# A fused gated recurrence and maxout layer: w_out fetched in two halves, and block 0's second layer split by unit halves around its first layer

## The chip, the cores and the metric

The kernel runs on one core of a Trainium2 chip. The metric is the device time of one launch in microseconds (us), as the median of repeated executions of the same program. Beside it there is one profiled execution with a trace of every instruction of the five engines: TensorE (PE, matrix products; PEld is its weight load), VectorE (DVE), ScalarE (ACT), GpSimd (POOL, here almost only an issuer of DMAs) and SyncE (SP, an issuer of DMAs).

## The reference

What is computed is a recurrence over time for each of four sequences of 6144 tokens and 256 channels, followed by a two-branch maxout layer on every token:

```python
sig = 1 / (1 + exp(-f_logit))
f = lower_bound + (1 - lower_bound) * sig
i = 1 - f
for t in range(S):                       # S = 6144, batch 4, 256 channels
    h = f[:, t] * h + i[:, t] * x[:, t]
    y[:, t] = h
h1 = y @ w1                              # 256 -> 1024
h2 = y @ w2
out = maximum(h1, h2) @ w_out            # 1024 -> 256
```

The kernel uses max(h1, h2) = h1 + relu(h2 - h1). So the first layer multiplies by wd, made of w2 - w1; the second layer multiplies the relu's result by w_out, and adds y times w13, the product of w1 and w_out, which is made once on the chip.

## The kernel before

Time is cut into blocks of 512 tokens. The 24576 tokens make 48 blocks; the first sequence begins with four blocks that are fetched singly (block 0 even in two halves by SP, lines 113 to 123), the rest in chunks of 1024 that go through a scratch buffer and are transposed by the DMA (`cross`, line 143). For each block:

- the gate: ACT takes the sigmoid of the turned logits (`gate`, L201; for block 0 inside `first_recurrence`, L252);
- the recurrence: DVE makes the decay (L207), the drive (L217) and scans them (L224; block 0 L258), which gives y with channels on the partitions;
- the first layer (`first_layer`, L434): 1024 units as eight groups `fc` of 128, two matmuls of 512 tokens each. Two groups share a PSUM tile `dT`, of which there are two in turn, and ACT's relu (L442) empties a tile into `rts`, half precision;
- the second layer (`second_layer`, L480): for each of four groups of 128 tokens, ten matmuls of 256 columns into one PSUM tile: two of y with `w13`, eight of the relu's groups with `wob` (w_out in half precision). When two token groups are done, ACT or DVE copies them to `osb` and SP stores the block (`store`, L453).

From block 4 on, pairs of blocks use seven products in place of eight for the second layer (`sevenths`, L643); that part isn't touched. Its parts t1 to t4 are made of `wob` and `w13` by `make_sevens` (L413).

The order of instructions on each engine is the order of the calls in the program, written out by hand; there is no scheduler. An engine runs its instructions in that order, and waits where an operand or a buffer isn't ready. PSUM has the two `dT` tiles (pool `ps_d`) and four `ps` tiles (pool `ps_o`).

The opening, lines 657 to 750, is where the change lies. In order:

- SP issues the loads of block 0 in two halves, then of w1 and w2, each in two halves `g` of 512 units (`fetch_w`): w1 half 0, w2 half 0, w1 half 1, w2 half 1.
- POOL waits for the first half of w1 (`pool_waits`, L341), then issues the load of w_out in one DMA (L666, it converts to half precision), the loads of blocks 1 to 3 (L105) and of the first scratch chunk (L100).
- PE keeps busy with transposes of a constant (`warm_up`, L678) between the turns of block 0's halves (L136).
- w1's half g is scaled (`scale_w1`, L345, ACT) and cast (`half_w1`, L349: half 0 on ACT, half 1 on DVE); PE turns it (`turn_w1`, L376), and DVE keeps the turned copy as `w1T` (`keep_w1T`, L382). `make_wd` (L358, DVE) makes the first-layer weights from w2 and the scaled w1, in pairs of unit groups.
- Block 0's first layer for units 0 to 3 needs half 0 alone, for units 4 to 7 half 1.
- `make_w13` (L390) is two products of eight matmuls, one for each 128 channels; ACT copies each to `w13` (L397).
- Block 1's logits and x are turned by PE (`turn`, L174), 8 transposes each; block 1's recurrence follows on ACT and DVE.
- Block 0's second layer runs as eight slots of five matmuls, between which stand block 2's turns and the first matmuls of block 1's first layer.

From block 2 on, PE alternates two matmuls of a block's first layer with five of the second layer of the block before.

Of the kernel before, what the change touches and what calls it, by code (L numbers as in the profile page):

```python
# [9 lines left out]
FP32 = mybir.dt.float32  # L10
# [8 lines left out]
def kernel(  # L19
# [76 lines left out]
    def fetch(c, s):  # L96
        b, t0, nt, _ = chunks[c]
        src = srcs[s][b, t0 : t0 + nt, :]
        if by_xbar(c, s):
            nc.gpsimd.dma_start(  # L100
                out=pieces(scratch[s][c % NSCR][:]), in_=pieces(src)
            )
        else:
            nat = inpool.tile([P, TB // P, D], HALF, name=("fT", "xT")[s])
            nc.gpsimd.dma_start(  # L105
                out=nat[:].rearrange("p i d -> p (i d)"),
                in_=src.rearrange("(p i) d -> p (i d)", p=P),
            )
            held[c, s] = nat
# [87 lines left out]
    def gate(j):  # L197
        new_mid(j, ("u",))
        u = mids[j, "u"]
        fT = turned[j, 0]  # L200
        nc.scalar.activation(  # L201
            out=like(u[:, :, 0:TB], fT), in_=fT, func=AF.Sigmoid, scale=-1.0
        )
# [40 lines left out]
    def first_recurrence(k):  # L244
        nt = TB // 2
        cols = slice(k * nt, (k + 1) * nt)
        if k == 0:
            new_mid(0, ("u", "ff", "v"))
            new_block(0)
        u, ff, v = (mids[0, t] for t in ("u", "ff", "v"))  # L250
        fT, xT = raws[k, 0], raws[k, 1]
        nc.scalar.activation(  # L252
            out=like(u[:, :, cols], fT), in_=fT, func=AF.Sigmoid, scale=-1.0
        )
        decay(ff, u, cols)
        drive(v, u, xT, cols)
        for h in range(KC):
            nc.vector.tensor_tensor_scan(  # L258
                out=y_of(0, h)[:, cols],
                data0=ff[:, h, cols],  # L260
                data1=v[:, h, cols],
                initial=y_of(0, h)[:, nt - 1 : nt] if k else 0.0,
                op0=ALU.mult,
                op1=ALU.add,
            )
# [49 lines left out]
    lbr = const.tile([KC, P], FP32)  # L315
    waited = const.tile([P, 1], FP32)
    warm = const.tile([P, 1], FP32)
    wob = wpool.tile([P, FC, D], HALF)
    wd = wpool.tile([P, KC, DFF], HALF)
    w1T = wpool.tile([P, FC, D], HALF)  # L320
    w13 = wpool.tile([P, KC, D], HALF)
# [18 lines left out]
    def pool_waits(t):  # L340
        nc.gpsimd.tensor_copy(out=waited[:], in_=t)  # L341

    def scale_w1(g):
        for kc in range(KC):
            nc.scalar.mul(w1s[g][:, kc, :], w1n[g][:, kc, :], om[:, kc : kc + 1])  # L345

    def half_w1(g, copy):
        for kc in range(KC):
            copy(out=w1h[g][:, kc, :], in_=w1s[g][:, kc, :])  # L349
# [19 lines left out]
        g, q = divmod(fc, NQ)  # L369
        return slice(g * NQ * P + q, (g + 1) * NQ * P, NQ)  # L370

    def turn_w1(g):
        pt = ps_o.tile([P, NQ, KC, P], HALF, name="ps")
        for q in range(NQ):
            for kc in range(KC):
                nc.tensor.transpose(  # L376
                    pt[:, q, kc, :], w1h[g][:, kc, q : NQ * P : NQ], ident[:]
                )
        return pt

    def keep_w1T(g, pt):
        nc.vector.tensor_copy(  # L382
            out=w1T[:, g * NQ : (g + 1) * NQ, :],
            in_=pt[:].rearrange("p q k d -> p q (k d)"),
        )

    def make_w13(kc):
        psw = ps_o.tile([P, 2, D], FP32, name="ps")
        for fc in range(FC):
            nc.tensor.matmul(  # L390
                psw[:, 0, :],
                lhsT=w1T[:, fc, kc * P : (kc + 1) * P],
                rhs=wob[:, fc, :],
                start=(fc == 0),
                stop=(fc == FC - 1),
            )
        nc.scalar.copy(out=w13[:, kc, :], in_=psw[:, 0, :])  # L397

# [1 line left out]

    def right(k, cols):

        return wob[:, k * KH : (k + 1) * KH, cols], w13[:, k, cols]

    def make_sevens():
        b11, b12, b21, b22 = (right(k, c) for k in range(2) for c in (lo, hi))
# [19 lines left out]
    def first_layer(j, fc):  # L428
        k, g = divmod(fc, KH)
        if fc % 2 == 0:  # L430
            dts["d"] = ps_d.tile([P, 2, TB], FP32, name="dT")
        dT = dts["d"]
        for kc in range(KC):
            nc.tensor.matmul(  # L434
                dT[:, fc % 2, :],
                lhsT=wd[:, kc, unit_cols(fc)],
                rhs=y_of(j, kc),
                start=(kc == 0),
                stop=(kc == KC - 1),
            )  # L440
        if fc % 2:
            nc.scalar.activation(  # L442
                out=rts[j, k][:, g - 1 : g + 1, :].rearrange(
                    "p q (i m) -> p q i m", m=P
                ),
                in_=dT[:].rearrange("p q (m i) -> p q i m", m=P),
                func=AF.Relu,
            )

    def store(j, osb, groups=slice(0, TB // P), cols=slice(0, D), queue=None):  # L450
        b, t0, nb, c, o = blocks[j]
        r0 = b * S + t0
        (queue or nc.sync).dma_start(  # L453
            out=out[r0 : r0 + nb, :].rearrange("(p n) d -> p n d", p=P)[
                :, groups, cols
            ],
            in_=osb[:, groups, cols],
        )
# [3 lines left out]
    def second_layer(j, slot):  # L462
        ns = TB // P
        n = KC + FC
        total = ns * n
        for k in range(slot * total // FC, (slot + 1) * total // FC):
            i, s = divmod(k, n)
            g, r = divmod(i, 2)
            if s == 0 and r == 0:
                acc["ps"] = ps_o.tile([P, 2, D], FP32, name="ps")  # L470
                if i == 0:
                    acc["osb"] = opool.tile([P, TB // P, D], FP32, name="osb")
            ps, osb = acc["ps"], acc["osb"]
            toks = slice(i * P, (i + 1) * P)
            if s < KC:
                left, right = y_of(j, s)[:, i:TB:ns], w13[:, s, :]
            else:
                fc = s - KC
                left, right = rts[j, fc // KH][:, fc % KH, toks], wob[:, fc, :]
            nc.tensor.matmul(  # L480
                ps[:, r, :],
                lhsT=left,
                rhs=right,
                start=(s == 0 and r == 0),
                stop=(s == n - 1 and r == 1),
                skip_group_check=True,
            )
            if r == 1 and s == n - 1:
                (nc.scalar.copy if j in (0, 3) else nc.vector.tensor_copy)(
                    out=osb[:, 2 * g : 2 * g + 2, :], in_=ps[:]  # L490
                )
                if i == ns - 1:
                    store(j, osb)

    sums = {}

# [160 lines left out]
    with tc.manual_schedule():  # L657
# [4 lines left out]
        fetch_first(1)  # L662
        for g in range(NG):
            fetch_w(g)
        pool_waits(w1n[0][:, 0, 0:1])
        nc.gpsimd.dma_start(  # L666
            out=wob[:].rearrange("p (g q) c -> p g (q c)", g=NG),
            in_=moe_w_out.rearrange("(g p q) c -> p g (q c)", g=NG, q=NQ),
        )
        for c in range(1, 5):  # L670
            for s in range(2):
                fetch(c, s)
        wt = ps_d.tile([P, 2, 2 * TB], HALF, name="dT")
        lbc = ps_d.tile([P, TB], FP32, name="dT")

        def warm_up(n):
            for q in range(n):
                nc.tensor.transpose(wt[:, 0, 0:P], ident[:], ident[:])  # L678
# [18 lines left out]
        first_turn(1, 0)  # L697
        first_turn(1, 1)
        first_recurrence(1)
        warm_up(24)  # L700
        scale_w1(0)
        half_w1(0, nc.scalar.copy)
        scale_w1(1)
        pt0 = turn_w1(0)
        for pair in range(2):
            make_wd(0, pair)
            for fc in range(2 * pair, 2 * pair + 2):
                first_layer(0, fc)
        half_w1(1, nc.vector.tensor_copy)
        pt1 = turn_w1(1)  # L710
        for pair in range(2):
            make_wd(1, pair)
            for fc in range(4 + 2 * pair, 6 + 2 * pair):
                first_layer(0, fc)
        keep_w1T(0, pt0)
        keep_w1T(1, pt1)
        steps = turn_steps(1)
        make_w13(0)
        turn(steps[:8])
        gate(1)  # L720
        make_w13(1)
        turn(steps[8:])
        for step in scan_steps(1):
            step()
        cross(4)
        for fc in range(FC):
            if fc == 4:
                turn(turn_steps(2))
                gate(2)
            if fc == 6:  # L730
                first_layer(1, 0)
                first_layer(1, 1)
            if fc < 7:
                second_layer(0, fc)
        for step in scan_steps(2):
            step()
        for step in make_sevens():
            step()
        for fc in range(2, FC):
            first_layer(1, fc)  # L740
            if fc == 3:
                second_layer(0, 7)
        turn(turn_steps(3))
        gate(3)
        early = scan_steps(3)
# [106 lines left out]
```

## Time and profile before

| | |
|---|---|
| median of 5 executions | 379.16 us |
| lowest to highest | 378.44 to 380.36 us |
| the profiled execution, its own time | 378.44 us |
| its span, first to last instruction | 376.7 us |
| time around the span | 1.7 us |
| mean granted clock of TensorE | 0.999 |
| DVE, ACT, POOL busy | 90%, 80%, 12% of the span |
| first matmul of block 0's first layer | 11.11 us |
| first matmul of block 2's first layer | 27.49 us |
| w_out, issue to landing | 6.2 us |

The profiled execution is the lowest of the five. Lines of the trace are read as: start, length, engine, source line, operation, what is written from what is read (buffer numbers left out), shapes, how many in a row; in brackets, how long the engine had been idle before and what ended that. A matmul's length covers its latency, and the next one starts before it ends, so the pace of PE is read from one start to the next.

### The profile page before, as it was taken

What the parts mean: (1) busy time and instruction counts of PE and PEld (TensorE: products, weight loads), DVE (VectorE), ACT (ScalarE), POOL (GpSimd) and SP (SyncE); (2) the same over time, 40 slices, a digit from 0 to 9 for tenths busy, and PEclk for the clock granted to TensorE, in tenths of its full rate; (3) what the DMA queues carried; (4) which work ended last, traced back from release to release, by engine and by line L of the source; (5) the groups of instructions that cost most, each with busy time, mean ns of one, the idle gap of its engine ahead of it and who ended that gap; (6) DMA issues with size and microseconds to landing.
All of it is one profiled execution on the core that took longest, in us unless ns stands there. A gap on an engine that the chain in (4) does not pass through costs nothing.

```text
span 376.7 us, 9634 instructions
## 1 busy us (share of the span) xinstructions
PE 369.4 (98%) x4156; PEld 281.9 (75%) x4156; DVE 338.1 (90%) x408; ACT 303.2 (80%) x412; POOL 43.6 (12%) x80
## 2 busy tenths in 40 slices
PE   7999999999999999999999999999999999999995
PEld 6777767777777777777777777777777777777784
DVE  5796889999999999999999999999999999999762
ACT  5866798888888798798888888887988888888752
POOL 1402101201102012011022021010110220110000
PEclk9999999999999999999999999999999999999999
DMA  8999979999999799799999998999997999992223
GB/s 267 241 209 233 271 131 221 220 178 269 211 140 260 126 273 240 158 279 198 195 238 211 197 292 140 218 276 140 258 274 143 250 219 180 232 183 86 114 111 114
DMA packets 104543, 77.17 MB, mean 205 GB/s; under 512 B 93298, under 2 KB 95348, under 8 KB 103796
## 3 DMA queue, kind: packets, MB, share of 16 engines
q1 hardware_dynamic: 101536, 51.19, 61.8%
q0 software_dynamic: 2544, 25.17, 35.4%
q8 instruction: 32, 0.52, 0.6%
q10 hardware_dynamic: 420, 0.20, 0.2%
q14 instruction: 11, 0.09, 0.1%
HBM read 53.48 MB, written 48.23 MB: 270 GB/s over the span
## 4 chain that ended last, share of the span: by engine, by line
PE 96%; DMA 1%; SPq 0%; DVE 0%; ACT 0%; issue 0%; DVEq 0%
PE ps L643 45%; PE dT L434 44%; PE ps L480 5%; DMA osb<-in_x_dram 1%; PE ps L174 1%; PE dT L678 1%; PE ps L390 0%; SPq L117 0%; PE ps L376 0%; DVE osb L561 0%; ACT nat L128 0%; PE ps L136 0%; DVE osb L582 0%; ACT sn L574 0%; PE dT L643 0%
## 5 line engine op out<-in xcount | busy, mean ns | idle before, releaser
L442 ACT ACTIVATE r<-dT 128x1024 f16<-128x1024 f32 x192 | 196.1, 1023 | 52.3 <-PE dT L434 52.1
L434 PE MATMUL dT<-r,wd 128*128 128x512 f16 x768 | 225.1, 379 | 0.0
L643 PEld LDWEIGHTS <-S 128*128 128x128 f16 x1760 | 115.5, 101 | 37.2 <-DVE S L499 0.2
L643 PEld LDWEIGHTS <-r 128*128 128x128 f16 x1320 | 90.9, 101 | 36.9 <-issue 0.2
L224 DVE TENSOR_TENSOR_SCAN r<-ff,r,v 128x512 f16<-128x512 f16 x88 | 108.2, 1269 | 0.8
L643 PE MATMUL ps<-t,S 128*128 128x128 f16 x1320 | 101.6, 219 | 0.0
L499 DVE TENSOR_TENSOR S<-r 128x2560 f16<-128x2560 f16 x44 | 65.4, 1487 | 14.3 <-ACT r L442 14.1
L434 PEld LDWEIGHTS <-wd 128*128 128x128 f16 x768 | 67.7, 113 | 4.8 <-DVE wd L358 0.6
L643 PE MATMUL ps<-wob,r 128*128 128x128 f16 x704 | 69.9, 219 | 0.0
L499 DVE TENSOR_TENSOR S<-r,S 128x2560 f16<-128x2560 f16 x44 | 64.9, 1475 | 0.0
L279 ACT ACTIVATE u<-fT 128x512 f16<-128x512 f16 x88 | 56.1, 637 | 1.3 <-DMA fT<-scr 1.3
L341 POOL CAST waited<-fT 128x1 f32<-128x1 f16 x22 | 17.8, 809 | 284.4 <-DMA fT<-scr 284.4
L207 DVE TENSOR_SCALAR ff<-u,nom 128x512 f16<-128x512 f16 (+1 forms) x98 | 31.8, 345 | 9.8 <-ACT u L279 3.9
L643 PE MATMUL ps<-w,r 128*128 128x128 f16 x176 | 38.5, 219 | 0.0
L643 PE MATMUL ps<-t,r 128*128 128x128 f16 x430 | 34.1, 219 | 0.1
L561 DVE TENSOR_TENSOR osb<-ps,sn 128x512 f32<-128x512 f32 x44 | 30.1, 684 | 3.2 <-PE ps L643 3.2
L643 PE MATMUL ps<-wob,S 128*128 128x128 f16 x352 | 32.6, 219 | 0.0
L217 DVE TENSOR_TENSOR v<-u,xT 128x1024 f16<-128x1024 f16 x44 | 30.1, 684 | 0.0
L549 ACT COPY sn<-ps 128x512 f32<-128x512 f32 x44 | 25.8, 586 | 2.0 <-PE ps L643 2.0
L559 ACT COPY osb<-ps 128x512 f32<-128x512 f32 x43 | 25.1, 583 | 0.8 <-PE ps L643 0.8
L480 PEld LDWEIGHTS <-r 128*128 128x128 f16 x160 | 16.0, 101 | 6.6
L643 PE MATMUL ps<-w,S 128*128 128x128 f16 x88 | 19.3, 219 | 0.0
(58 smaller groups left out, 136.2 us busy)
## 6 DMA issues: line engine op xcount, KB each, us to landing
out_dram<-osb SPq DMA_DIRECT2D x46, 512.0 KB, 4.3
scr<-in_f_logit_dram POOLq DMA_DIRECT2D x22, 512.0 KB, 7.5
scr<-in_x_dram POOLq DMA_DIRECT2D x22, 512.0 KB, 10.3
r<-in_moe_w_dram SPq DMA_DIRECT2D x4, 512.0 KB, 6.4
fT<-in_f_logit_dram POOLq DMA_DIRECT2D x3, 256.0 KB, 8.3
xT<-in_x_dram POOLq DMA_DIRECT2D x3, 256.0 KB, 8.9
out_dram<-osb SPq DMA_DIRECT2D x3, 256.0 KB, 2.5
osb<-in_f_logit_dram SPq DMA_DIRECT2D x2, 256.0 KB, 3.0
```

What stands on the lines that cost most here:

```text
L207: nc.vector.tensor_scalar(out=ff[:, h, cols], in0=u[:, h, cols], scalar1=nom[:, h : h + 1], scalar2=1.0, op0=ALU.mult, op1=ALU.add,)
L217: nc.vector.tensor_tensor(out=like(v[:, :, cols], xT), in0=like(u[:, :, cols], xT), in1=xT, op=ALU.mult,)
L224: nc.vector.tensor_tensor_scan(out=y_of(j, h), data0=ff[:, h, o : o + TB], data1=v[:, h, o : o + TB], initial=0.0 if t0 == 0 else y_of(j - ...
L279: nc.scalar.activation(out=mids[p + NBLK, "u"][:, h, cols], in_=held[c, 0][:, h, cols], func=AF.Sigmoid, scale=-1.0,)
L434: nc.tensor.matmul(dT[:, fc % 2, :], lhsT=wd[:, kc, unit_cols(fc)], rhs=y_of(j, kc), start=(kc == 0), stop=(kc == KC - 1),)
L442: nc.scalar.activation(out=rts[j, k][:, g - 1 : g + 1, :].rearrange("p q (i m) -> p q i m", m=P), in_=dT[:].rearrange("p q (m i) -> p q i ...
L480: nc.tensor.matmul(ps[:, r, :], lhsT=left, rhs=right, start=(s == 0 and r == 0), stop=(s == n - 1 and r == 1), skip_group_check=True,)
L499: nc.vector.tensor_tensor(out=t[:], in0=a, in1=b, op=op)
L549: nc.scalar.copy(out=t[:], in_=bank[b][:])
L559: nc.scalar.copy(out=dst, in_=bank[b][:])
L561: nc.vector.tensor_tensor(out=dst, in0=bank[b][:], in1=snap[name][:], op=ALU.add)
L643: nc.tensor.matmul(bank[b][:, i, :], lhsT=a[:, k, cols], rhs=w, start=fresh, stop=after is not None, skip_group_check=True,)
```

## The change

Four things change, all in the opening.

1. `wob` becomes two tiles, one for each half of the units, each loaded by a DMA of its own. POOL waits for block 0's second gate (the last column of the first half of `mids[0, "u"]`) in place of the first half of w1, and the loads that POOL issues come after that point.
2. The scaling of w1's half 1 moves from ACT, where it stood ahead of block 0's relus, to DVE, after the turned half 0 has been kept. `keep_w1T` of each half moves ahead.
3. Block 0's second layer runs in a new function, `second_first`: after the first layer's units 0 to 3 it multiplies their relu with the first half of w_out for all four token groups, into two PSUM tiles that stay open; only then is half 1 of w1 turned and are units 4 to 7 computed. The y part and units 4 to 7 follow after `make_w13`, for three token groups in a row and a fourth after block 2's logits have been turned. Both copies to `osb` are ACT's. The relu of units 6 and 7 of block 0 moves to DVE.
4. `make_w13` writes both its products into one `dT` tile in place of two `ps` tiles; the order of it, of block 1's turns and of block 2's turns changes as shown. Block 1's first layer runs its units 2 to 7 without second-layer matmuls between.

```diff
-    wob = wpool.tile([P, FC, D], HALF)
+    wob = [wpool.tile([P, KH, D], HALF, name=f"wob{g}") for g in range(2)]
...
-    def scale_w1(g):
+    def scale_w1(g, mul):
         for kc in range(KC):
-            nc.scalar.mul(w1s[g][:, kc, :], w1n[g][:, kc, :], om[:, kc : kc + 1])
+            mul(w1s[g][:, kc, :], w1n[g][:, kc, :], om[:, kc : kc + 1])
...
     def make_w13(kc):
-        psw = ps_o.tile([P, 2, D], FP32, name="ps")
+        if kc == 0:
+            dts["w"] = ps_d.tile([P, 2, TB], FP32, name="dT")
+        psw = dts["w"][:, kc, :]
         for fc in range(FC):
             nc.tensor.matmul(
-                psw[:, 0, :],
+                psw[:, 0:D],
                 lhsT=w1T[:, fc, kc * P : (kc + 1) * P],
-                rhs=wob[:, fc, :],
+                rhs=wob[fc // KH][:, fc % KH, :],
                 start=(fc == 0),
                 stop=(fc == FC - 1),
             )
-        nc.scalar.copy(out=w13[:, kc, :], in_=psw[:, 0, :])
+        nc.scalar.copy(out=w13[:, kc, :], in_=psw[:, 0:D])
...
         if fc % 2:
-            nc.scalar.activation(
...
-                func=AF.Relu,
-            )
+            dst = rts[j, k][:, g - 1 : g + 1, :].rearrange("p q (i m) -> p q i m", m=P)
+            src = dT[:].rearrange("p q (m i) -> p q i m", m=P)
+            if j == 0 and fc == FC - 1:
+                nc.vector.tensor_scalar_max(out=dst, in0=src, scalar1=0.0)
+            else:
+                nc.scalar.activation(out=dst, in_=src, func=AF.Relu)
...
+    def open_first():
+        acc["first"] = [ps_o.tile([P, 2, D], FP32, name="ps") for g in range(2)]
+        acc["osb0"] = opool.tile([P, TB // P, D], FP32, name="osb")
+
+    def second_first(i, fcs, y=False):
+        ns = TB // P
+        g, r = divmod(i, 2)
+        ps, osb = acc["first"][g], acc["osb0"]
+        toks = slice(i * P, (i + 1) * P)
+        terms = [(y_of(0, s)[:, i:TB:ns], w13[:, s, :]) for s in range(KC) if y]
+        terms += [
+            (rts[0, fc // KH][:, fc % KH, toks], wob[fc // KH][:, fc % KH, :])
+            for fc in fcs
+        ]
+        for n, (left, right) in enumerate(terms):
+            nc.tensor.matmul(
+                ps[:, r, :],
+                lhsT=left,
+                rhs=right,
+                start=(fcs[0] == 0 and r == 0 and n == 0),
+                stop=(fcs[-1] == FC - 1 and n == len(terms) - 1),
+                skip_group_check=True,
+            )
+        if fcs[-1] == FC - 1 and r == 1:
+            nc.scalar.copy(out=osb[:, 2 * g : 2 * g + 2, :], in_=ps[:])
+            if i == ns - 1:
+                store(0, osb)
...
-        pool_waits(w1n[0][:, 0, 0:1])
-        nc.gpsimd.dma_start(
-            out=wob[:].rearrange("p (g q) c -> p g (q c)", g=NG),
-            in_=moe_w_out.rearrange("(g p q) c -> p g (q c)", g=NG, q=NQ),
-        )
-        for c in range(1, 5):
-            for s in range(2):
-                fetch(c, s)
...
         first_recurrence(1)
+        pool_waits(mids[0, "u"][:, 0, TB - 1 : TB])
+        for g in range(NG):
+            nc.gpsimd.dma_start(
+                out=wob[g][:].rearrange("p q c -> p (q c)"),
+                in_=moe_w_out[g * NQ * P : (g + 1) * NQ * P, :].rearrange(
+                    "(p q) c -> p (q c)", q=NQ
+                ),
+            )
+        for c in range(1, 5):
+            for s in range(2):
+                fetch(c, s)
         warm_up(24)
-        scale_w1(0)
+        scale_w1(0, nc.scalar.mul)
         half_w1(0, nc.scalar.copy)
-        scale_w1(1)
         pt0 = turn_w1(0)
         for pair in range(2):
             make_wd(0, pair)
             for fc in range(2 * pair, 2 * pair + 2):
                 first_layer(0, fc)
+        keep_w1T(0, pt0)
+        scale_w1(1, nc.vector.tensor_scalar_mul)
         half_w1(1, nc.vector.tensor_copy)
-        pt1 = turn_w1(1)
+        pt1 = new_pt()
+        open_first()
+        for fcs in ((0, 1), (2, 3)):
+            for i in range(TB // P):
+                second_first(i, fcs)
+        turn_w1(1, pt1)
         for pair in range(2):
             make_wd(1, pair)
+            if pair:
+                keep_w1T(1, pt1)
             for fc in range(4 + 2 * pair, 6 + 2 * pair):
                 first_layer(0, fc)
-        keep_w1T(0, pt0)
-        keep_w1T(1, pt1)
         steps = turn_steps(1)
-        make_w13(0)
         turn(steps[:8])
         gate(1)
+        make_w13(0)
+        turn(steps[8:])
         make_w13(1)
-        turn(steps[8:])
         for step in scan_steps(1):
             step()
         cross(4)
-        for fc in range(FC):
-            if fc == 4:
-                turn(turn_steps(2))
-                gate(2)
-            if fc == 6:
-                first_layer(1, 0)
-                first_layer(1, 1)
-            if fc < 7:
-                second_layer(0, fc)
+        last = tuple(range(KH, FC))
+        for i in range(3):
+            second_first(i, last, True)
+        steps = turn_steps(2)
+        turn(steps[:8])
+        gate(2)
+        second_first(3, last, True)
+        first_layer(1, 0)
+        first_layer(1, 1)
+        turn(steps[8:])
         for step in scan_steps(2):
             step()
         for step in make_sevens():
             step()
         for fc in range(2, FC):
             first_layer(1, fc)
-            if fc == 3:
-                second_layer(0, 7)
```

More of the change, by code (lines that the diff above doesn't have):

```diff
@@ L370, in unit_cols, with new_pt, turn_w1 @@
         return slice(g * NQ * P + q, (g + 1) * NQ * P, NQ)
-    def turn_w1(g):
-        pt = ps_o.tile([P, NQ, KC, P], HALF, name="ps")
+    def new_pt():
+        return ps_o.tile([P, NQ, KC, P], HALF, name="ps")
+    def turn_w1(g, pt=None):
+        pt = pt or new_pt()
         for q in range(NQ):
@@ L396, in make_w13 @@
             )
-        nc.scalar.copy(out=w13[:, kc, :], in_=psw[:, 0, :])
+        nc.scalar.copy(out=w13[:, kc, :], in_=psw[:, 0:D])
     lo, hi = slice(0, P), slice(P, 2 * P)
     def right(k, cols):
-        return wob[:, k * KH : (k + 1) * KH, cols], w13[:, k, cols]
+        return wob[k][:, :, cols], w13[:, k, cols]
     def make_sevens():
@@ L441, in first_layer @@
         if fc % 2:
[L442 to L446, printed above, removed]
-                func=AF.Relu,
-            )
+            dst = rts[j, k][:, g - 1 : g + 1, :].rearrange("p q (i m) -> p q i m", m=P)
[4 more added lines that the diff above has]
+                nc.scalar.activation(out=dst, in_=src, func=AF.Relu)
     def store(j, osb, groups=slice(0, TB // P), cols=slice(0, D), queue=None):
@@ L478, in second_layer @@
                 fc = s - KC
-                left, right = rts[j, fc // KH][:, fc % KH, toks], wob[:, fc, :]
+                left, right = rts[j, fc // KH][:, fc % KH, toks], wob[fc // KH][:, fc % KH, :]
             nc.tensor.matmul(
@@ L488, in second_layer @@
             if r == 1 and s == n - 1:
-                (nc.scalar.copy if j in (0, 3) else nc.vector.tensor_copy)(
+                (nc.scalar.copy if j == 3 else nc.vector.tensor_copy)(
                     out=osb[:, 2 * g : 2 * g + 2, :], in_=ps[:]
```

## The prediction

> **What bounds the kernel now.** I read the page first: its busy shares, then the chain that ended last.
>
> ```profile
> PE 369.4 (98%) x4156; PEld 281.9 (75%) x4156; DVE 338.1 (90%) x408; ACT 303.2 (80%) x412; POOL 43.6 (12%) x80
> ...
> PE 96%; DMA 1%; SPq 0%; DVE 0%; ACT 0%; issue 0%; DVEq 0%
> ```
>
> PE is 98% busy, and 96% of the chain is PE work. A busy PE need not be PE at its peak, so I next read PE's order of time over the opening, where the change sits (start us, length, instruction, count; starts minus starts give the pace).
>
> ```profile
> 10.46 0.81 PE L376 MATMUL ps<-ident,S 128*128 128x128 f16 x8
> 11.11 1.91 PE L434 MATMUL dT<-r,wd 128*128 128x512 f16 x8
> 12.85 0.61 PE L376 MATMUL ps<-ident,S 128*128 128x128 f16 x8
> 13.30 1.98 PE L434 MATMUL dT<-r,wd 128*128 128x512 f16 x8
> 15.12 1.06 PE L390 MATMUL ps<-wob,w1T 128*128 128x256 f16 x8
> 16.02 0.61 PE L174 MATMUL ps<-ident,fT 128*128 128x128 f16 x8
> 16.46 1.04 PE L390 MATMUL ps<-wob,w1T 128*128 128x256 f16 x8
> 17.34 0.61 PE L174 MATMUL ps<-ident,xT 128*128 128x128 f16 x8
> 17.78 0.49 PE L480 MATMUL ps<-w,r 128*128 128x256 f16 x2
> ...
> 27.49 0.59 PE L434 MATMUL dT<-r,wd 128*128 128x512 f16 x2
> ```
>
> Eight L434 take 12.85 - 11.11 = 1.74, 0.217 each; eight L390 0.87, 0.109 each; eight transposes 0.44. From 12.85 to 27.49 (block 2's first matmul) work stands back to back. I count only some 0.25 us lost: 0.09 in the second L434 group, 0.03 after each L390 group, 0.11 at 17.78, where the second matmul waits for w13. So reordering can recover at most 0.25 there and 0.16 at 10.46 (the transposes wait for ACT's S): 0.4 us, 0.1% of the run.
>
> ACT and DVE beside it, then POOL:
>
> ```profile
> 10.84 1.34 ACT L345 ACTIVATE r<-r,om 128x512 f32<-128x512 f32 x2 [0.20 <-DMA r<-in_moe_w_dram]
> 12.19 1.94 ACT L442 ACTIVATE r<-dT 128x1024 f16<-128x1024 f32 x2
> ...
> 17.58 0.37 ACT L397 CAST w<-ps 128x256 f16<-128x256 f32 x1
> ```
>
> ```profile
> 10.40 1.65 DVE L358 SCALAR_TENSOR_TENSOR wd<-r,om 128x256 f16<-128x256 f32 x4
> 11.98 0.74 DVE L349 CAST S<-r 128x512 f16<-128x512 f32 x2
> 12.65 1.66 DVE L358 SCALAR_TENSOR_TENSOR wd<-r,om 128x256 f16<-128x256 f32 x4
> 14.24 1.27 DVE L382 COPY w1T<-ps 128x1024 f16<-128x1024 f16 x2
> ```
>
> ```profile
> 8.44 0.87 POOL L666 DMA_DIRECT2D wob<-in_moe_w_out_dram  x1
> ...
> 14.94 0.50 POOL L100 DMA_DIRECT2D scr<-in_x_dram  x1 [1.57 <-DMA wob<-in_moe_w_out_dram]
> ```
>
> The reader should see: the first relu starts at 12.19 and a relu takes 1.02 (pitch 0.92); w1's second half has just landed at 10.84; w_out, issued at 8.44, lands 6.2 later (14.64), first needed at 15.12.
>
> **What the Trainium skill says.** "TensorE: Matmul & The Clock Gate", Back-to-back issue gap: N/2.4 + 2.5 ns when warm, 216 ns for 512 columns and 109 for 256; the trace agrees (217, 109). So moving matmuls changes no price. "VectorE: DVE Perf Modes", The perf-mode tier table: tensor_scalar on fp32 in SBUF runs at twice the base rate, with an fp32 PSUM operand at the base rate; the errata table above it gives 120 + FD cycles at 0.96 GHz from PSUM. The trace agrees for the like of both: DVE's fp32 cast of 512 (L349) takes 0.41, and L217 reading 1,024 from PSUM 1.22. "DMA: Bandwidth & Descriptors", Issuing engines are not separate DMA queues: all DMAs share 16 engines and interleave. The trace shows the sharing, though little interleaving at first: between 8 and 10 us the SP queue alone fills 105% of them, and POOL's w_out packets first appear after 10.25.
>
> **The change, part by part.** PE's matmuls are the same: block 0's second layer was 40 of L480, and is 16 + 24. So the sum is of waits added and removed, on the clock of the profiled execution. Until 12.85 nothing differs: warm_up(24), the turn of w1's first half and units 0-3 keep their places, and relu 0-1 waits for its matmuls (4 issued by 11.76, the last ending 0.38 later, 12.14), so taking L345 off ACT gains it 0.05 at most.
>
> 1. First half amid the first layer. At 12.85 PE turned w1's second half; now it wants relu 0-1: 12.18 + 1.02 = 13.20, issue 13.25. Wait 0.40. Eight matmuls to 14.12; relu 2-3 ends 13.10 + 1.02 = 14.12: wait 0.05. Eight more to 15.04.
>
> 2. w_out. POOL now waits for block 0's second gate (ACT 7.35, 0.59 long: 7.94) instead of w1 (8.30), so the issue starts at about 8.15, and each half takes about the 0.55 of an fT issue. Queued behind it on POOL: the six fT/xT fetches, shifted under 0.3, and block 1's fT is needed at 17.23 instead of 16.02. Half 0's landing is not in the trace. Upper bound: whole w_out's landing, 14.64, less the second half's 0.26 MB at the 0.43 MB per 2 us that POOL's queue moves from 12 to 14 us (1.2): 13.45. Lower: less also the 0.6 by which its issue ends earlier (8.70 for 9.31), if the engines take it up at once: 12.85. Needed 13.25. I take a wait of 0.1 beyond step 1 (0 to 0.25).
>
> 3. w1's second half on DVE. After wd (11.98): keep_w1T 0.60 (half of 1.27 less overlap), scale two at pitch 0.34 as L349, or 0.6 if at base rate, cast 0.67: S ready at 14.0 to 14.5; PE turns it at 15.04. No wait. wd pair 0 by 14.8 to 15.3, first layer needs it at 15.48; pair 1 by 15.6 to 16.1, needed 16.35. Free, by up to 0.2. keep_w1T of half 1 ends about 16.4, before 17.67. Units 4-7: 15.48 to 17.23.
>
> 4. Relu 6-7 on DVE: matmuls end at 17.39, (120 + 1,024)/0.96 = 1.19 by the skill's table (L217 1.22), done 18.65. Next there is block 1's decay, which waits for gate(1) until 18.9. Hidden; if it grew by over 0.25 it would push block 1's scans, which end at 23.2 against a need at 23.64.
>
> 5. w13. Turn f 17.23-17.67; make_w13(0) 17.67-18.54; turn x to 18.98. Both products now use one dT tile, and in the changed program's instruction list the second product's first matmul waits for ACT's copy of the first. ACT: gate(1) from 17.87, pitch 0.92, copy 18.79-19.16. PE resumes 19.21: wait 0.23. make_w13(1) then issues to 20.08, ends 20.24; copy 20.28-20.65. In the kernel before, eight transposes covered this copy (17.34-17.78, and still 0.11 waited). Now second_first follows directly; only one y matmul (w13's first half) can go ahead, so the second issues at 20.70: wait 0.51. Seventeen more matmuls to 22.55.
>
> 6. Turn f(2) to 22.99, second_first(3) to 23.64, block 1 units 0-1 to 24.51, turn x(2) to 24.95. gate(2) follows the first osb copy, 23.2; second osb copy 24.12; relu 0-1 24.67; units 2-3 issue to 25.82, relu 2-3 26.02-27.04. Units 4-5 go to 26.69; units 6-7 need the dT buffer that relu 2-3 frees: 27.08, wait 0.39. Before, L480 work between the pairs (23.14, 24.33) hid this. Then to 27.95, turn(3) to 28.84, block 2 starts.
>
> Stores: block 0's leaves from the same place in SP's queue; cross(4)'s transposes still wait for the same two scr loads. DVE afterwards: scans of block 2 end 28.9, the sevens (1.95) 30.85, block 3's scans about 35.7, needed at 36.64. Late, not on the path.
>
> Sum: added 0.40 + 0.05 + 0.10 + 0.23 + 0.51 + 0.39 = 1.68; removed 0.25. Net +1.4 (28.84 - 27.49 = 1.35 without the w_out term). PE is full from there to the end, so nothing recovers it. The profiled execution took 378.44, 376.7 of it span; it becomes 379.9. It is the lowest of five, 0.72 under their median of 379.16; against the median the same 1.4 gives 380.6.
>
> **Rivals.**
> - Not slower: the executions that the profile doesn't show. Before, w1's second half was awaited by ACT at 10.84, and S was done 0.13 before PE wanted it (12.72 to 12.85): a landing over about 0.13 later stalls PE. After, S has 0.5 to 1 to spare. If that is what makes the median 0.72 longer than the profiled run, the change returns it: 380.6 - 0.7 = 379.9, no measurable change; at the highest run's 1.92, 378.7, faster. For it: the spread of the runs, and both cover margins. Against: w_out's half 0 is equally tight after, at 13.25, and w_out itself had only 0.5 before.
> - Half 0 of w_out is late: it shares engines with w1 and w2, and if it lands only with the whole at 14.64, PE waits 1.4 at 13.25 instead of 0.05 to 0.4; +1.1 more, 381.7. For: the SP queue is served until about 12. Against: half the bytes come first.
> - The waits don't carry: PE later proves paced by DVE (90% busy) or by buffers, and absorbs the shift: 379.2. For: DVE above 95% in the 200-300 us stage. Against: PE's busy equals the span in every stage from 13 to 300 us. I put unknown effects of either sign here too.
>
> **How the numbers follow.** Main case 0.50: 380.6, own range 380.0 to 381.2. Not slower by better cover 0.22, late half 0.15, no carry or unknown 0.13. A measurement tells about 0.3%, 1.14 us, from no change: slower means above 380.30. Main case: 0.36 slower, 0.14 within. Cover: 0.17 within, 0.05 faster. Late half: 0.15 slower. Last: 0.07 within, 0.06 faster. Together faster 0.11, same 0.38, slower 0.51. The range 379.2 to 381.7 holds all of the main case, most of the cover case and the smaller late halves, 0.8 in all.
>
> **What would show it.** In the changed profile: PE waits on ACT's relu before the first second-layer matmul (0.4), on a w13 copy between the two products (0.2) and after the second (0.5), and on relu 2-3 before block 1's units 6-7 (0.4); block 2's first matmul at 28.8 to 29.0 instead of 27.49; S on DVE before 14.6. A wait named w_out above 0.3 is the late half. If block 2 starts within 0.3 of 27.49, or if the end is not shifted as block 2's start is, my sum is wrong.

## The result, and the profile after

The changed kernel takes 380.24 us (median of 43 executions, 379.25 to 383.76), the kernel before 379.28 us in the comparison (80 executions, 377.9 to 382.71). The ratio is 1.0025, with a 95% interval of 1.0013 to 1.0038: slower, by 0.96 us, where 1.4 was forecast. The interval is 0.5 to 1.44 us, so it just holds the forecast as well.

The profiled execution of the changed kernel took 382.14 us and is one of its longest. Its span is 380.3. Its page, with busy time and the chain that ended last:

```profile
PE 368.3 (97%) x4156; PEld 280.5 (74%) x4156; DVE 340.3 (89%) x411; ACT 301.2 (79%) x409; POOL 42.9 (11%) x81
...
DMA 57%; PE 34%; issue 3%; POOL 2%; DVE 1%; ACT 1%; SPq 0%; POOLq 0%; DVEq 0%
```

The chain has turned from 96% PE to 57% DMA, and that misleads. Followed back from the end it reaches one place near 292 us where PE waited for a DVE copy that was late behind a chunk's x (the first line below is PE's waits after 45 us, the second DVE's order of time):

```profile
PE ps L677 <- DVE osb L595: 1.1, 1, 1.1
```

```profile
287.44 0.69 DVE L217 TENSOR_TENSOR v<-u,xT 128x1024 f16<-128x1024 f16 x1 [2.50 <-DMA xT<-scr]
```

From there the chain follows scratch transfers back to the start, although PE waited for none of the others. It is one late transpose (8.97 us from its issue, where the median of all 22 is 5.2), and hardly a trait of the changed kernel: a variant of the kernel before, with another input for block 1, had such a wait too, of 1.5 us. So the profile of the changed kernel was taken once more among the experiments, and that one is read here. It took 379.99 us, its span is 378.2. PE's order of time over the opening:

```profile
11.19 1.89 PE L439 MATMUL dT<-r,wd 128*128 128x512 f16 x8
13.46 1.91 PE L516 MATMUL ps<-wob,r 128*128 128x256 f16 x16 [0.39 <-DMA wob<-in_moe_w_out_dram]
15.21 0.61 PE L379 MATMUL ps<-ident,S 128*128 128x128 f16 x8
15.65 1.89 PE L439 MATMUL dT<-r,wd 128*128 128x512 f16 x8
17.38 0.61 PE L174 MATMUL ps<-ident,fT 128*128 128x128 f16 x8
17.83 1.04 PE L395 MATMUL dT<-wob,w1T 128*128 128x256 f16 x8
18.70 0.61 PE L174 MATMUL ps<-ident,xT 128*128 128x128 f16 x8
19.37 1.03 PE L395 MATMUL dT<-wob,w1T 128*128 128x256 f16 x8
20.24 0.27 PE L516 MATMUL ps<-w,r 128*128 128x256 f16 x1
20.86 0.27 PE L516 MATMUL ps<-w,r 128*128 128x256 f16 x1 [0.35 <-ACT w L402]
...
25.12 1.89 PE L439 MATMUL dT<-r,wd 128*128 128x512 f16 x8
27.26 1.02 PE L439 MATMUL dT<-r,wd 128*128 128x512 f16 x4 [0.25 <-ACT r L452]
...
29.02 0.59 PE L439 MATMUL dT<-r,wd 128*128 128x512 f16 x2
```

The reader is to see the gaps by adding the pace to a start. Eight L439 from 11.19 are issued by 12.93, the next matmul starts at 13.46: 0.53 lost. Eight transposes from 18.70 are issued by 19.15, the second product starts at 19.37: 0.22. The first y matmul at 20.24 is issued by 20.35, the second starts at 20.86: 0.51. Eight L439 from 25.12 are issued by 26.86, the next start at 27.26: 0.40. (The brackets give less than the gap, since the busy time of a matmul covers its latency.) Three numbers of a profile are used from here on:

- the start: the first matmul of block 0's first layer;
- the stretch: from there to the first matmul of block 2's first layer (29.02 here), which holds every edit on PE (one edit moves a wait to just behind it, as will be seen);
- the rest: from there to the end of the span.

| | start | stretch | rest |
|---|---|---|---|
| before, profile of 378.44 us | 11.11 | 16.38 | 349.21 |
| changed, profile of 382.14 us | 11.17 | 18.86 | 350.27 |
| changed, profile of 379.99 us | 11.19 | 17.83 | 349.18 |

The rest is the same to 0.03 in the first and third row: in these profiles nothing of what the opening loses comes back, and nothing is lost later. In the second row the 1.1 of the late transpose is in it, and the stretch has 1.0 more because w_out's first half landed late (matmuls at 14.48 instead of 13.46).

### The profile page after: what moved, and what is told of

It is laid out like the page before. It is cut to its first block, busy times and chain, and to the rows that moved or that the text cites. A ratio compares the mean times of both kernels' runs of the same rounds, so it can differ in the third digit from the quotient of the medians.

```text
span 380.3 us, 9635 instructions
## 1 busy us (share of the span) xinstructions
PE 368.3 (97%) x4156; PEld 280.5 (74%) x4156; DVE 340.3 (89%) x411; ACT 301.2 (79%) x409; POOL 42.9 (11%) x81
## 4 chain that ended last, share of the span: by engine, by line
DMA 57%; PE 34%; issue 3%; POOL 2%; DVE 1%; ACT 1%; SPq 0%; POOLq 0%; DVEq 0%
DMA fT<-scr 25%; DMA scr<-in_f_logit_dram 24%; PE dT L439 15%; PE ps L677 13%; PE ps L484 3%; DMA scr<-in_x_dram 3%; DMA xT<-scr 2%; DMA wob<-in_moe_w_out_dram 2%; POOL waited L341 2%; DMA osb<-in_x_dram 1%; PE ps L516 1%; PE ps L174 1%; DVE r L224 0%; DVE osb L595 0%; SPq L117 0%
## 5 line engine op out<-in xcount | busy, mean ns | idle before, releaser
L439 PE MATMUL dT<-r,wd 128*128 128x512 f16 x768 | 225.0, 379 | 0.2 <-ACT r L452 0.2
L677 PEld LDWEIGHTS <-r 128*128 128x128 f16 x1320 | 90.9, 101 | 38.0 <-issue 1.5
L439 PEld LDWEIGHTS <-wd 128*128 128x128 f16 x768 | 67.6, 113 | 5.2 <-issue 0.5
L484 PEld LDWEIGHTS <-r 128*128 128x128 f16 x120 | 12.1, 101 | 5.8
```

Of the source, the lines that this page charges most:

```text
L439: nc.tensor.matmul(dT[:, fc % 2, :], lhsT=wd[:, kc, unit_cols(fc)], rhs=y_of(j, kc), start=(kc == 0), stop=(kc == KC - 1),)
L677: nc.tensor.matmul(bank[b][:, i, :], lhsT=a[:, k, cols], rhs=w, start=fresh, stop=after is not None, skip_group_check=True,)
```

## The experiments

Kernels of one group ran on the same chip and share the executions of the kernel before there, whose median was 378.45 us in the first group, 379.13 in the second and 379.59 in the third. These differ by more than the effects, so ratios and stretches are compared, not medians across groups. (A ratio given here is not exactly that of the two medians.)

### One wait at a time

First edit, in `second_first`, the y terms behind the unit terms:

```diff
-        terms = [(y_of(0, s)[:, i:TB:ns], w13[:, s, :]) for s in range(KC) if y]
-        terms += [
+        terms = [
             (rts[0, fc // KH][:, fc % KH, toks], wob[fc // KH][:, fc % KH, :])
             for fc in fcs
         ]
+        terms += [(y_of(0, s)[:, i:TB:ns], w13[:, s, :]) for s in range(KC) if y]
```

> The changed kernel with the y terms behind the unit terms in second_first, so that four matmuls stand between the second make_w13 and its first use. Sum of waits: the wait for w13 after the second product (0.51 in the changed kernel's profile, 21.36 to 21.87) falls to 0.1 or less, block 2's first matmul comes 0.4 to 0.5 earlier on an equal landing of w_out, and the time is 0.4 to 0.5 under the changed kernel, so about 0.5 over the kernel before (ratio 1.0013). If waits in the opening are given back later: the wait goes and the time stays at about 0.95 over the kernel before (ratio 1.0025).

Measured: 379.55 us, ratio 1.0023 (1.0014 to 1.0031). PE in its profile:

```profile
18.98 1.03 PE L395 MATMUL dT<-wob,w1T 128*128 128x256 f16 x8
19.85 0.60 PE L516 MATMUL ps<-wob,r 128*128 128x256 f16 x4
20.29 0.46 PE L516 MATMUL ps<-w,r 128*128 128x256 f16 x2
20.58 0.60 PE L516 MATMUL ps<-wob,r 128*128 128x256 f16 x4
```

Four matmuls now stand between the product and its use, and the two of w13 take 0.29 instead of 0.22: 0.07 waited, 0.44 less than before the edit. The stretch is 17.51 and not 17.83 - 0.44 = 17.39, because the first second-layer matmul stood 2.37 after the start (13.06 - 10.69) where the repeated profile has 2.27; within the eight first-layer matmuls from 10.69 PE had waited some 0.2 for wd. The ratio lies above the 1.0013 expected and among those of the unedited kernel (1.0025 and 1.0027), so the gain of 0.4 is shown in the profile alone; the timing can't tell it.

Second edit, a tile of its own for each product:

```diff
-        if kc == 0:
-            dts["w"] = ps_d.tile([P, 2, TB], FP32, name="dT")
-        psw = dts["w"][:, kc, :]
+        psw = ps_d.tile([P, 2, TB], FP32, name="dT")[:, 0, :]
```

> The changed kernel with a PSUM tile of its own for the second product of make_w13. Sum of waits: the 0.23 wait between the second turn of block 1 and the second product goes; the copies of w13 end 0.2 earlier, and the time is 0.2 under the changed kernel, 0.7 over the kernel before (ratio 1.002). If the wait was for something else than the copy of the first product (the gate of block 1 on ACT, say), the second product still starts at least 0.2 after the turn's last matmul was issued.

Measured: 380.29 us, ratio 1.0037 (1.0023 to 1.0051), stretch 17.69.

```profile
18.45 0.61 PE L174 MATMUL ps<-ident,xT 128*128 128x128 f16 x8
18.89 1.04 PE L393 MATMUL dT<-wob,w1T 128*128 128x256 f16 x8
```

The second product follows the turn after 0.44, the pace of eight transposes: the wait of 0.22 is gone, so it was for the shared tile. Again no gain can be read from the timing.

Third edit, block 3's logits turned between the pairs:

```diff
         for fc in range(2, FC):
+            if fc == 6:
+                steps = turn_steps(3)
+                turn(steps[:8])
             first_layer(1, fc)
-        turn(turn_steps(3))
+        turn(steps[8:])
```

> The changed kernel with the turn of block 3's logits (8 transposes, 0.44) put between units 4-5 and 6-7 of block 1's first layer. Sum of waits: the wait of 0.25 to 0.39 for relu 2-3 in front of units 6-7 goes, and the time is 0.3 to 0.4 under the changed kernel, 0.6 over the kernel before (ratio 1.0015). If the relus pace this stretch however PE's work is ordered, the wait returns in front of block 2's first matmul and nothing is won.

Measured: 379.89 us, ratio 1.0029 (1.0017 to 1.0041), stretch 17.34.

```profile
24.99 1.89 PE L439 MATMUL dT<-r,wd 128*128 128x512 f16 x8
26.71 0.61 PE L174 MATMUL ps<-ident,fT 128*128 128x128 f16 x8
27.16 1.03 PE L439 MATMUL dT<-r,wd 128*128 128x512 f16 x4
28.02 0.61 PE L174 MATMUL ps<-ident,xT 128*128 128x128 f16 x8
28.47 0.87 PE L439 MATMUL dT<-r,wd 128*128 128x512 f16 x2
29.17 0.38 PE L484 MATMUL ps<-w,r 128*128 128x256 f16 x2
```

No gap is left from 24.99 to 28.47: the wait was for want of other PE work between the pairs. But most of it returns just behind block 2's first matmul, where the stretch ends. The two L439 from 28.47 should be issued by 28.90, and the next matmul starts at 29.17: 0.27 lost (in the unedited kernel 29.02 is followed by 29.45, without loss). The second of the two reads the second half of block 2's y, and DVE's scan of it ends at 26.45 + 2.46 = 28.91:

```profile
26.45 2.46 DVE L224 TENSOR_TENSOR_SCAN r<-ff,r,v 128x512 f16<-128x512 f16 x2
```

So of the 0.40 that this edit wins on PE, 0.27 goes to the next wait, for DVE. The stretch leaves that out, here and in the later versions that hold this edit (28.67 to 29.37, 27.10 to 27.80 and 27.07 to 27.77: 0.27 each).

Fourth edit, the first half without w_out:

```diff
-            (rts[0, fc // KH][:, fc % KH, toks], wob[fc // KH][:, fc % KH, :])
+            (
+                rts[0, fc // KH][:, fc % KH, toks],
+                wob[1][:, fc % KH, :] if fc >= KH else wd[:, fc % KC, 0:D],
+            )
```

> The changed kernel, but the first half of block 0's second layer multiplies the relu with columns of wd (made by 12.1) in place of the first half of w_out, so that this step doesn't wait for w_out; block 0's output is thereby another one. Late w_out theory: in most executions w_out's first half lands near 14.4, as in the changed kernel's profile, and the wait at 12.9 falls from 1.58 to 0.45 (relu 0-1 alone); the time is about 1.1 under the changed kernel, at or under that of the kernel before (ratio 0.9995). Sum of waits as predicted (w_out costs 0 to 0.25 beyond the relu in a typical execution, and the profiled one was late): the time is 0 to 0.25 under the changed kernel, ratio 1.002.

Measured: 380.33 us, ratio 1.0045 (1.0025 to 1.0064): no faster than the others, above what either theory had, and the 0.9995 of the late w_out lies outside the interval. So the late landing of the first profile is not what a typical execution pays. The profiles agree: in seven of them w_out's first half is needed at this place, and the first second-layer matmul stands 2.14 to 2.37 after the start in six, and 3.31 only in the first.

```profile
11.64 1.89 PE L439 MATMUL dT<-r,wd 128*128 128x512 f16 x8
13.79 1.96 PE L519 MATMUL ps<-wd,r 128*128 128x256 f16 x16 [0.25 <-ACT r L452]
15.59 0.61 PE L379 MATMUL ps<-ident,S 128*128 128x128 f16 x8
```

It isolates the relu's wait: 13.79 - 11.64 - 1.74 = 0.41 ahead of the first matmul, and 15.59 - 13.79 - 1.74 = 0.06 within. The stretch is 17.75, so w_out cost the repeated profile of the changed kernel 0.1. This execution starts late, at 11.64, since w1's first half landed late; that lies outside the edits.

### All of them, and parts alone

The changed kernel again:

> The changed kernel once more, beside the others on one chip. Sum of waits: from block 0's first first-layer matmul to block 2's 17.75 us when w_out's first half lands by 13.3 (16.38 in the kernel before), up to 1.1 more when it lands near 14.4; the median 1.35 to 1.6 over the kernel before (ratio 1.0036 to 1.0042). If something in the change is given back in typical executions: ratio 1.0025 or under, as measured first, with the stretch of 17.75 all the same.

Measured: 380.12 us, ratio 1.0027 (1.0014 to 1.0039), stretch 17.83. The stretch is that of the sum. The ratio is nearer to the rival's, but its interval reaches the 1.0036 of the sum. A give-back is thus suggested, not shown, and the first group speaks against a general one: there, where the kernel before had a median of 378.45, the four edited kernels were 0.9, 1.4, 1.1 and 1.7 us over it by their ratios, and their stretches were 1.1, 1.3, 1.0 and 1.4 over 16.38.

The three edits together (the diffs above):

> The changed kernel with all three edits of the first experiments (y terms last, a tile of its own for the second product, block 3's logits turned between units 4-5 and 6-7). Sum of waits: the gains add, 0.43 + 0.23 + 0.39, the stretch is 16.7, and the time is 0.3 to 0.4 over the kernel before (ratio 1.001), what is left being the wait for relu 0-1 and, where late, w_out. If the waits stand in for each other (one removed, the next grows), the stretch stays above 17.

Measured: 379.29 us, ratio 1.0005 (0.9989 to 1.0020), stretch 16.88. In the stretch the gains add: 17.83 to 16.88 is 0.95 of the 1.05 expected. With the 0.27 behind it counted, 0.68 is left.

The same with the first half moved behind the whole first layer:

```diff
-            if j == 0 and fc == FC - 1:
+            if False:
...
+        scale_w1(1, nc.scalar.mul)
         pt0 = turn_w1(0)
...
-        keep_w1T(0, pt0)
-        scale_w1(1, nc.vector.tensor_scalar_mul)
         half_w1(1, nc.vector.tensor_copy)
-        pt1 = new_pt()
-        open_first()
-        for fcs in ((0, 1), (2, 3)):
-            for i in range(TB // P):
-                second_first(i, fcs)
-        turn_w1(1, pt1)
+        pt1 = turn_w1(1)
         for pair in range(2):
             make_wd(1, pair)
-            if pair:
-                keep_w1T(1, pt1)
             for fc in range(4 + 2 * pair, 6 + 2 * pair):
                 first_layer(0, fc)
+        keep_w1T(0, pt0)
+        keep_w1T(1, pt1)
+        open_first()
+        for fcs in ((0, 1), (2, 3)):
+            for i in range(TB // P):
+                second_first(i, fcs)
```

> The kernel of the three edits, and the first half of block 0's second layer moved behind the whole of its first layer, with w1's second half scaled on ACT, turned before it and the relu of units 6-7 on ACT, as in the kernel before; w_out still in two DMAs and the second layer still in halves. Sum of waits: nothing is waited for, the stretch is 16.2 to 16.4, and the time is that of the kernel before within 0.3 (ratio 0.9993 to 1.0007). If working by halves or the two DMAs cost by themselves: 0.5 or more over the kernel before.

Measured: 378.58 us, ratio 0.9987 (0.9972 to 1.0002), stretch 16.51, a little over the range expected. Not every wait is gone: PE waits 0.17 for block 1's x in the stretch and 0.27 for DVE's scan just behind it. But halves and the two DMAs don't cost the 0.5 of the rival; it was the placing. The interval just reaches 1, so a gain over the kernel before isn't shown.

Of the change, w_out's part alone on the kernel before:

```diff
-        pool_waits(w1n[0][:, 0, 0:1])
-        nc.gpsimd.dma_start(
...
+        pool_waits(mids[0, "u"][:, 0, TB - 1 : TB])
+        for g in range(NG):
+            nc.gpsimd.dma_start(
```

> The kernel before with w_out in two DMAs that wait for block 0's gate, and nothing else of the change. Sum of waits: the first product needs half 0 at 15.1 and half 1 at 15.6, the halves land between 13.0 and 15.9; the time is that of the kernel before, at most 0.3 more (ratio 1.0000 to 1.0008). If the earlier issue delays w1 and w2: block 0's first first-layer matmul comes later than 11.1, and the time is 0.5 or more over the kernel before.

Measured: 378.62 us, ratio 0.9992 (0.9970 to 1.0014), start 10.90: no cost is shown, and w1 isn't delayed in the profile. But its stretch is 17.54, with the work of the kernel before in the order of the kernel before:

```profile
16.31 1.04 PE L390 MATMUL ps<-wob,w1T 128*128 128x256 f16 x8
18.37 0.62 PE L174 MATMUL ps<-ident,xT 128*128 128x128 f16 x8 [1.02 <-DMA xT<-in_x_dram]
```

Eight L390 from 16.31 are issued by 17.18; PE waits 1.19 there for block 1's x, which the first profile of the kernel before had by 17.34. That gave the third group its question.

### Does the kernel before wait for loads that the changed one needs later?

A second profile of the kernel before, without an edit:

> The kernel before once more, for a second profile of it. Cover theory: if the execution is longer than 378.44, PE waits in the opening for the inputs of block 1 (fT at 16.0 or xT at 17.3), and the stretch from block 0's to block 2's first first-layer matmul is longer than 16.38 by that wait; if the stretch is 16.4 and the execution is long all the same, the spread comes from later. Ratio 1 by its nature.

Measured: 379.43 us, ratio 1.0001 (0.9969 to 1.0033); the profiled execution took 379.55.

```profile
15.62 1.03 PE L390 MATMUL ps<-wob,w1T 128*128 128x256 f16 x8 [0.36 <-DMA wob<-in_moe_w_out_dram]
16.89 0.62 PE L174 MATMUL ps<-ident,fT 128*128 128x128 f16 x8 [0.24 <-DMA fT<-in_f_logit_dram]
17.35 1.04 PE L390 MATMUL ps<-wob,w1T 128*128 128x256 f16 x8
18.41 0.62 PE L174 MATMUL ps<-ident,xT 128*128 128x128 f16 x8
```

The same 11.12 start as in the first profile, but PE stands still for w_out (15.62 against 15.12 before), for block 1's logits (15.62 + 0.87 = 16.49 to 16.89) and for its x (17.35 + 0.87 = 18.22 to 18.41). Block 2 starts at 28.48, the stretch is 17.36 and the rest 349.32. So of this execution's 1.1 over 378.44, 0.98 lies in the opening, in these waits, and 0.1 in the rest.

Both kernels with block 1's turns reading block 0's inputs, which are there:

```diff
-        raws[k, s] = nat
+        raws[k, s] = nats[k, s] = nat
...
+                            (
+                                nats[q // 2, s][:, q % 2, h * P : (h + 1) * P]
+                                if j == 1
-                            held[c, s][:, q, h * P : (h + 1) * P],
+                                else held[c, s][:, q, h * P : (h + 1) * P]
+                            ),
```

> The kernel before, but the turns of block 1 read block 0's inputs (already in SBUF) in place of the inputs loaded for block 1; the loads are still issued, and the first sequence's outputs from block 1 on are other ones. Cover theory: typical executions of the kernel before wait for block 1's x (1.0 us in the profile of the one with w_out alone changed), so this kernel's median falls by 0.5 to 1.2 below the kernel before (ratio 0.997 to 0.9987), towards that one's shortest executions. If the spread of the executions comes from elsewhere (the chunks' transposes later, w1's landing): no difference, ratio 0.9995 to 1.0005.

> The changed kernel with the same edit: block 1's turns read block 0's inputs. Cover theory: the changed kernel needs block 1's inputs 1.2 to 1.5 later and seldom waits for them, so this kernel is within 0.3 of the changed kernel, 0.7 to 1.0 over the kernel before (ratio 1.002 to 1.0027), and 1.3 to 1.7 over the kernel before with the same edit, as the sum of waits has it. If both kernels wait for these loads alike, it falls by as much as the kernel before does.

Measured: the kernel before with this edit 378.92 us, ratio 0.9991 (0.9975 to 1.0007); the changed kernel with it 379.91 us, ratio 1.0012 (0.9994 to 1.0030). Both missed what the cover theory gave them. The first lies between the ranges of the two theories, with an interval that holds 1. The second lies under its range, and against the 1.0027 of the changed kernel as it is (on another chip) it fell by 0.0015, no less than the kernel before did by 0.0009; this is what the rival had, that both kernels wait alike. The intervals are too wide to settle it. The two profiles, in which nothing waits for block 1's inputs, have stretches of 16.62 and 17.93: 1.31 apart, as the sum has it, where the medians are 0.99 apart. The first of them lost 1.5 us later on, behind a late chunk (`PE ps L648 <- DVE osb L566: 1.5, 1, 1.5`).

Last, the version with the first half behind the first layer, and block 1's inputs ahead of w_out's second half:

```diff
+            if g == 0:
+                for s in range(2):
+                    fetch(1, s)
-        for c in range(1, 5):
+        for c in range(2, 5):
```

> The kernel in which no wait of the sum was left (first half behind the first layer, y terms last, own tile, block 3's turn between), with block 1's inputs loaded ahead of w_out's second half. Cover theory: block 1's x lands about 1.2 earlier and isn't waited for, w_out's second half is needed at 17.2 and lands by 16.5; the time is 0.2 to 0.8 under the kernel before (ratio 0.998 to 0.9995). Without it: the same time as that kernel had with the loads in the old order, ratio 0.9987 within its interval.

Measured: 378.91 us, ratio 0.9994 (0.9974 to 1.0013), stretch 16.49 with no wait for x in its profile (17.81 after 16.94, the pace of eight products). It isn't shown to be faster than the kernel before, nor than the version in the old order of loads.

## Why the prediction was right, and where its size was off

- **Nothing to win on PE.** Right as far as tried: the version with the first half behind the first layer, 0.9987 (0.9972 to 1.0002), is the best that any order reached here, and isn't shown to be faster.
- **Relu ahead of the first half, 0.40 + 0.05.** Shown by the kernel without w_out there: 0.41 and 0.06.
- **w_out's first half, 0.1 (0 to 0.25).** Right in six of seven profiles, 0.1 in the repeated one; the upper bound was too narrow for the seventh, the first, where the half landed at 14.44 by the chain (8.15 and 6.29 after), as the rival of the late half has it (a stretch of 1.0 more).
- **w1's second half on DVE.** Right, free: S was done at 13.87 in the repeated profile, and PE turned it at 15.21. The two scalings took 0.79 from start to start of what follows (12.33 to 13.12), where the prediction had 0.68 at the doubled rate and 1.2 at the base rate. The Trainium skill, "VectorE: DVE Perf Modes", The perf-mode tier table, gives the doubled rate for this operation on fp32 in SBUF, and the trace is nearer to it.
- **Relu 6-7 on DVE.** Right: 1.23 against 1.19, and DVE then still waited 0.28 for the gate of block 1.
- **The shared tile, 0.23, and w13 after the second product, 0.51.** 0.22 and 0.51; each went with its own edit.
- **Units 6-7 of block 1, 0.39.** 0.40; it went with other work between, but 0.27 of it came back as a wait for DVE's scan of block 2. The prediction had that scan end at 28.9, late but "not on the path", with block 2 at 28.84: true of the changed kernel, with 0.2 to spare in the repeated profile.
- **Nothing recovered later.** Right: the rest is 349.21 and 349.18, and 349.0 to 349.6 in the other profiles without a late transpose. The rival in which DVE or buffers absorb the shift is refuted in the profiles.

The sum came out at a stretch of 17.83 against 16.38, 1.45 where 1.45 was summed (1.35, and 0.1 for w_out). So the mechanism was right. The forecast was 1.4 on the median and the median moved by 0.96. That is under the 1.14 which the prediction took as the least difference that a measurement tells, and its interval, 0.5 to 1.44, holds 1.4; the shortfall may be noise. If it is real, the step that was off is "against the median the same 1.4 gives 380.6". The profile of 378.44 us was an execution of the kernel before in which every load of the opening arrived in time; the removed term of 0.25 was counted there. In the second profile it would be 0.25 + 0.98. The rival "not slower" named such a give-back, of 0.7, but put it on w1's second half; PE turned that without a wait in all three profiles with the order of the kernel before (at 12.85, 12.84 and 12.62). The loads that were late are w_out and block 1's inputs, which the changed kernel needs later: block 1's logits at 17.38 instead of 16.02, its x at 18.70 instead of 17.34, w_out's first half alone being needed earlier.

That such waits occur is shown by two profiles of three. That they are what takes 1.45 down to 0.96 in the median is not. It fits that the shortest executions of the two kernels are 1.35 apart (377.9 and 379.25), as summed, and the medians less. It fits, too, that nothing was given back on the chip where the kernel before was at its fastest (378.45). But chips differ in more than these waits, and the test by medians was inconclusive, if anything against it. The cause of the shortfall stays open.

## What to carry to other kernels

Where PE is full, a reordering can only be priced by its waits: list for each moved step what its first instruction waits for, and what had stood between producer and consumer; such waits, read off one trace, gave the stretch to 0.1 us where w_out was not late. When a wait is removed, look behind the mark where you stop counting: 0.27 of one gain of 0.40 was lost again two matmuls on. Then ask which loads the one profiled execution had only just in time: a profile that is among the shortest executions can hide waits that others pay (0.98 here). And a second product written to the same PSUM tile waits for the copy of the first, even where it goes to the other half (0.22 here).

## What the runs showed of the hardware

The same load can take 1.5 us longer in one profile than in another. Block 1's x took 7.3 us from issue to landing in the first profile of the kernel before, 8.5 in the second and 8.8 with w_out in two DMAs. The start of the first layer moved between 10.58 and 11.79 us over the profiles with the landing of block 0's inputs and w1, and in two profiles a chunk's x came late enough to hold PE for 1.1 and 1.5 us, near no edit at all. All of it is of the size of the effect, which is why the stretch between two instructions of one engine told more than the time of the whole.
